# Moving the rows, the activations g, the outputs and the weight temporaries 320 bytes up in SBUF

## The chip, the cores and the metric

The kernel runs on one NeuronCore of a Trainium2 chip. The metric is the device time of one execution in microseconds, lower is better. Three executions of the kernel before took 889.12, 889.74 and 889.91 us; their median, 889.74 us, is the time before. A further execution was taken with the hardware profiler, and the rows further down come from it.

## What is computed

Attention within chunks of 64 positions, followed by a feed-forward layer. All numbers are float32.

```python
scores = q_c @ k_c.T / sqrt(64)          # per batch (8), head (8), chunk of 64 of 576 positions
attn   = exp(scores - max) / (sum + 1e-9)
x      = (attn @ v_c)                    # gathered to [4608 tokens, 512]
h      = x @ w_in                        # w_in  [512, 2048]
g      = h * sigmoid(1.702 * h)
out    = g @ w_out                       # w_out [2048, 512]
```

The weights come in as float64 words of 8 bytes, and the kernel makes float32 values from them itself.

## The kernel before, in words

The 4608 tokens are 36 tiles of 128 rows (`u`), and four tiles make a block (`n`, nine blocks of 512 tokens). The hidden width 2048 is 16 slices of 128 (`j`). The feed-forward part is 9 x 16 = 144 steps (`g = 16 n + j`), all built alike.

To keep float32 accuracy every factor is split in two float32r parts, a high one (`x_h`, `g_h`, plane 0 of `w`) and the rest (`x_l`, `g_l`, plane 1 of `w`), and three products are added. A step therefore has 24 matmuls of 128 x 128 x 512 on TensorE:

- `h_pe` (L606 to L608): four slices `cc` of the model width, three matmuls each, all into one PSUM tile `hp`. The stationary operand, which a weight load (LDWEIGHTS, engine PEld) brings in ahead of each matmul, is a 128-column slice of `w`; the moving operand is `x_l` or `x_h`.
- `g_hi` on ScalarE: L627 applies the activation to `hp` in place, L628 copies it to `g_h`. `g_lo` on VectorE, L632, writes `g_l = hp - g_h`.
- `o_pe` (L641 to L643): four token tiles `t`, three matmuls each, into four PSUM tiles `po`. Here the stationary operand is a 128-column (512-byte) slice of `g_l` or `g_h`, and the moving operand is `w`.

`g_h` and `g_l` have two buffers each, which the steps use in turn. After the last `j` of a block `o_out` copies `po` to `ob` and `o_store` stores it.

The attention of the tiles ahead and the preparation of the weights lie between these matmuls: q and k rows arrive in `rows` or `raw` (`load_rows` L231, `load_qk` L392), weights in `raw_j` (L163, L168). A weight slice passes through a temporary `wtmp` with three buffers (L181, L182 and L188 on VectorE write it, L193 and L196 read it). `s_max` takes the maximum of each score row into a small tile `m` and subtracts it (L451 to L456); `s_sum` makes `z` and `r`.

`Plan.emit` fixes the order of the instructions of all engines from costs written in the kernel, before any tile has an address. The addresses come from tile pools in the order of first use: a pool `const` first, then `two` (two buffers per tag: `xh`, `xl`, `m`, `z`, `r`, `raw`, `gh`, `gl`, `ob`), then `more` (`wtmp`).

Of the kernel before, what the change touches and what calls it, by code (L numbers as in the profile page):

```python
# [9 lines left out]
F32 = mybir.dt.float32  # L10
# [88 lines left out]
def tile_chunk_attention_ffn(  # L99
# [14 lines left out]
    P = 128  # L114
# [15 lines left out]
    two = ctx.enter_context(tc.tile_pool(name="two", bufs=2))  # L130
# [238 lines left out]
    def plan_pair(u):  # L369
# [3 lines left out]
        NG = 2 * NP * 2  # L373

        def bc(a):
            return a.unsqueeze(2).broadcast_to([P, NG, CH])
# [70 lines left out]
        def s_max():  # L447
            sc = st["s"]
            st["e"] = e = const.tile([P, NG, CH], F32, tag="e", name=f"e_{u}")
            m = two.tile([P, NG], F32, tag="m", name=f"m_{u}")  # L450
            nc.vector.tensor_reduce(m, sc, axis=AX.X, op=ALU.max)  # L451
            if pe:
                nc.vector.tensor_tensor(e, sc, bc(m), op=ALU.subtract)
            else:
                split = lambda a: a.rearrange("p (g h) j -> p g h j", h=2)
                nc.vector.tensor_tensor(split(e), sc, split(bc(m)), op=ALU.subtract)  # L456
# [96 lines left out]
        for t in range(2):  # L553
# [5 lines left out]
            PE, 2.4 if pe else 1.4, rank + 0.6, s_pe, need=need, make=ev("s"), take=["att", "att"], give=["tr"],  # L559
        )  # L560
        plan.add(DVE, 2.46, rank + 0.6, s_max, need=[ev("s")], make=ev("m"), take=["e"], give=["att", "att"])
        plan.add(ACT, 1.05, rank + 0.6, s_exp, need=[ev("m")], make=ev("ex"), table="exp")
        plan.add(DVE, 1.65, rank + 0.6, s_sum, need=[ev("ex")], make=ev("z"))
# [180 lines left out]
```

## Time and profile before

| What | Value |
|---|---|
| Median of three runs | 889.74 us |
| Profiled execution, its own time | 889.83 us |
| Span of that execution in the trace | 888.1 us |
| Time outside the span | 1.7 us |
| TensorE busy | 870.6 us, 98% |
| VectorE busy | 389.8 us, 44% |
| ScalarE busy | 317.6 us, 36% |
| GpSimd busy | 32.4 us, 4% |

The span is the time from the first to the last instruction of the program that the profiler saw. Matmuls are pipelined and their ends are modelled, so the time that a matmul takes from the stream is read from the distance between the starts of two matmuls, not from its listed length.

### The profile page before, as it was taken

How to read it: one execution, taken by the hardware profiler on the slowest of the kernel's cores; microseconds unless marked ns; L12 is line 12 of the kernel's file. 1: busy time of each engine (PE TensorE's matmuls, PEld its weight loads, DVE VectorE, ACT ScalarE, POOL GpSimd, SP SyncE). 2: the span in 40 equal slices, each digit the busy share in tenths (PEclk: the TensorE clock that was granted, in tenths of full speed). 3: DMA queues.
4: the chain of work that ended last, by engine and by line, in shares of the span. 5: the costliest groups of instructions: out<-in, count | busy, mean ns of one | idle time of the engine just before them, and what ended most of it. 6: DMA issues, size and time to landing. Idle time of an engine off the chain costs nothing.

```text
span 888.1 us, 14202 instructions
## 1 busy us (share of the span) xinstructions
PE 870.6 (98%) x5882; PEld 705.6 (79%) x5882; DVE 389.8 (44%) x511; ACT 317.6 (36%) x459; POOL 32.4 (4%) x24
## 2 busy tenths in 40 slices
PE   6799999999999999999999999999999999999998
PEld 5587888888888888888888888888888888888886
DVE  5899975277716153433535171617151411111111
ACT  3999653253423223232423241324232322222221
POOL 1000000011000000000000000000000000000000
PEclk9699999999999999999999999999999999999999
DMA  9995244233442313221222031102010110001001
GB/s 238 311 323 169 47 73 98 38 54 67 82 86 54 54 25 76 45 48 25 69 39 49 16 92 25 25 1 71 2 25 1 32 40 1 0 1 48 1 0 48
DMA packets 194592, 55.47 MB, mean 62 GB/s; under 512 B 179680, under 2 KB 187872, under 8 KB 194528
## 3 DMA queue, kind: packets, MB, share of 16 engines
q1 hardware_dynamic: 194528, 54.57, 26.3%
q8 instruction: 46, 0.75, 0.4%
q14 instruction: 18, 0.15, 0.1%
HBM read 45.09 MB, written 9.44 MB: 61 GB/s over the span
## 4 chain that ended last, share of the span: by engine, by line
PE 94%; SPq 2%; DMA 2%; ACT 1%; issue 0%; DVE 0%; ACTq 0%
PE po L641 16%; PE po L642 15%; PE po L643 15%; PE hp L608 15%; PE hp L607 15%; PE hp L606 15%; PE s L443 2%; PE x L503 2%; SPq L231 1%; DMA raw<-in_moe_w_in_dram 1%; DMA rows<-in_k_dram 1%; ACT raw L172 0%; PE qkTp L410 0%; SPq L168 0%; SPq L163 0%
## 5 line engine op out<-in xcount | busy, mean ns | idle before, releaser
L632 DVE TENSOR_TENSOR g_l<-hp,g_h 128x512 fp32r<-128x512 f32 x144 | 99.3, 690 | 413.3 <-ACT g_h L628 412.7
L641 PE MATMUL po<-w,g_l 128*128 128x512 f32 x576 | 232.1, 403 | 0.1
L628 ACT ACTIVATE g_h<-hp 128x512 fp32r<-128x512 f32 x144 | 86.3, 599 | 404.3 <-PE po L643 403.6
L642 PE MATMUL po<-w,g_h 128*128 128x512 f32 x576 | 227.7, 395 | 0.0
L643 PE MATMUL po<-w,g_h 128*128 128x512 f32 x576 | 227.7, 395 | 0.0
L608 PE MATMUL hp<-x_h,w 128*128 128x512 f32 x572 | 225.2, 394 | 0.0
L607 PE MATMUL hp<-x_h,w 128*128 128x512 f32 x572 | 223.9, 391 | 0.0
L606 PE MATMUL hp<-x_l,w 128*128 128x512 f32 x572 | 223.9, 391 | 0.0
L643 PEld LDWEIGHTS po<-w,g_h 128*128 128x128 f32 x576 | 108.6, 189 | 26.3
L641 PEld LDWEIGHTS po<-w,g_l 128*128 128x128 f32 x576 | 108.2, 188 | 25.4 <-DVE g_l L632 0.9
L606 PEld LDWEIGHTS hp<-x_l,w 128*128 128x128 f32 x572 | 107.8, 189 | 25.0
L642 PEld LDWEIGHTS po<-w,g_h 128*128 128x128 f32 x576 | 109.0, 189 | 23.5
L607 PEld LDWEIGHTS hp<-x_h,w 128*128 128x128 f32 x572 | 107.4, 188 | 25.1
L608 PEld LDWEIGHTS hp<-x_h,w 128*128 128x128 f32 x572 | 107.3, 188 | 23.6 <-DVE w L196 0.2
L627 ACT ACTIVATE hp<-hp 128x512 f32<-128x512 f32 x144 | 84.3, 585 | 72.6 <-PE hp L608 67.6
L490 DVE STREAM_TRANSPOSE eT<-e 32x512 f32<-32x512 f32 x112 | 78.7, 702 | 21.0 <-PE x L503 17.2
L470 POOL TENSOR_TENSOR e<-e,r 128x1024 f32<-128x1024 f32 x14 | 26.7, 1906 | 611.4 <-DVE r L466 325.5
L425 DVE STREAM_TRANSPOSE qkT<-raw 128x1024 f32<-128x1024 f32 x28 | 34.7, 1241 | 13.8 <-PE s L443 11.3
L515 ACT ACTIVATE x_h<-x 128x512 fp32r<-128x512 f32 x32 | 17.5, 595 | 33.2 <-PE x L503 33.1
L459 ACT ACT_TABLE_LOAD x16 | 20.5, 1283 | 19.0 <-DVE e L456 18.3
L463 DVE TENSOR_REDUCE z<-e 128x16 f32<-128x1024 f32 x16 | 19.5, 1218 | 9.5 <-ACT e L459 8.8
L443 PEld LDWEIGHTS s<-qkT 64*64 64x64 f32 x1024 | 18.2, 135 | 5.8 <-issue 5.8
(64 smaller groups left out, 412.2 us busy)
## 6 DMA issues: line engine op xcount, KB each, us to landing
out_dram<-ob SPq DMA_DIRECT2D x36, 256.0 KB, 2.1
raw<-in_moe_w_in_dram SPq DMA_DIRECT2D x16, 512.0 KB, 7.3
raw<-in_moe_w_out_dram SPq DMA_DIRECT2D x16, 512.0 KB, 8.0
v<-in_v_dram SPq DMA_DIRECT2D x28, 256.0 KB, 3.3
raw<-in_q_dram SPq DMA_DIRECT2D x144, 32.0 KB, 2.1
raw<-in_k_dram SPq DMA_DIRECT2D x144, 32.0 KB, 2.1
raw<-in_q_dram SPq DMA_DIRECT2D x48, 24.0 KB, 1.9
raw<-in_k_dram SPq DMA_DIRECT2D x48, 24.0 KB, 1.9
```

The costliest lines, as they stand in the source:

```text
L425: nc.vector.transpose(st["tr"][:, i].rearrange("p n (t j) -> p (n t) j", j=32), st["raw"][:, i].rearrange("p n t j -> p (n t) j"),)
L443: nc.tensor.matmul(o, tr[r, 0, n, cols], tr[r, 1, n, cols], start=True, stop=True)
L490: nc.vector.transpose(st["et"][po : po + 32, :, 32 * a : 32 * a + 32], st["e"][pi : pi + 32, :, 32 * b : 32 * b + 32],)
L606: nc.tensor.matmul(hp, wh, xl, start=cc == 0, stop=False)
L607: nc.tensor.matmul(hp, wh, xh, start=False, stop=False)
L608: nc.tensor.matmul(hp, wl, xh, start=False, stop=cc == NCC - 1)
L627: nc.scalar.activation(h_t[g], h_t[g], AF.Gelu_apprx_sigmoid)
L628: nc.scalar.activation(gh, h_t[g], AF.Copy)
L632: nc.vector.tensor_tensor(gl, h_t.pop(g), gh.bitcast(F32), op=ALU.subtract)
L641: nc.tensor.matmul(po, gl[:, c], w[:, 0, :], start=j == 0, stop=False)
L642: nc.tensor.matmul(po, gh[:, c], w[:, 0, :], start=False, stop=False)
L643: nc.tensor.matmul(po, gh[:, c], w[:, 1, :], start=False, stop=j == NF - 1)
```

## The change

The tile `m` of the paired tiles (`plan_pair`) asks for 56 columns in place of 16, and only its first 16 are used. That makes each of its two buffers 160 bytes per partition longer.

```diff
         def s_max():
             sc = st["s"]
             st["e"] = e = const.tile([P, NG, CH], F32, tag="e", name=f"e_{u}")
-            m = two.tile([P, NG], F32, tag="m", name=f"m_{u}")
+            m = two.tile([P, NG + 40], F32, tag="m", name=f"m_{u}")
+            m = m[:, :NG]
             nc.vector.tensor_reduce(m, sc, axis=AX.X, op=ALU.max)
```

The built program has the same 7171 instructions before and after, in the same order on each engine, with the same shapes and the same waits and semaphore updates. What differs is where some tiles start within each partition, in bytes:

| Tile (buffers) | Before | After |
|---|---|---|
| `w`, `raw_j`, the first tiles' `first_a`, `first_b` | 1664 + multiples of 8192 | the same |
| `qkT`, `v`, `e`, `eT` | 116352, 140928, 145024, 149120 | the same |
| `x_h`, `x_l` | 153216, 161408; 169600, 177792 | the same |
| `m` | 185984, 186048 | 185984, 186208 |
| `z`, `r` | 186112, 186176; 186240, 186304 | 320 higher |
| `rows` / `raw` | 186368, 194560 | 186688, 194880 |
| `g_h` | 202752, 204800 | 203072, 205120 |
| `g_l` | 206848, 208896 | 207168, 209216 |
| `ob` | 210944, 212992 | 211264, 213312 |
| `wtmp` | 215040, 219136, 223232 | 215360, 219456, 223552 |

From `rows` on, the moved tiles started at multiples of 2048 bytes (`rows` at 186368 = 91 x 2048); the unmoved ones from `w` to `x_l` start 128 bytes past a multiple of 512. After the change the moved tiles start 320 bytes past a multiple of 2048, which is 64 bytes past a multiple of 128 and of 256.

## Rows read from the trace of the kernel before

**Rows 1.** The page: the span and the instructions.

```profile
span 888.1 us, 14202 instructions
```

**Rows 2.** Windows: length, busy time (count) by engine, clock, DMA share, GB/s.

```profile
41.00:120.00 79.00, 78.69 (x586) 63.91 (x585) 74.81 (x83) 64.00 (x77) 0.00 (x0) 1.00 0.62 175
120.00:700.00 580.00, 580.00 (x4083) 468.67 (x4082) 254.36 (x341) 185.83 (x276) 26.68 (x14) 1.00 0.23 47
700.00:888.00 188.00, 184.35 (x854) 149.37 (x852) 32.35 (x48) 42.69 (x73) 0.00 (x0) 1.00 0.05 18
```

**Rows 3.** The page: the chain that ended last, by engine.

```profile
PE 94%; SPq 2%; DMA 2%; ACT 1%; issue 0%; DVE 0%; ACTq 0%
```

**Rows 4.** Waits: who waited for whom, us in total, times, longest.

```profile
DVE g_l L632 <- ACT g_h L628: 412.7, 102, 4.9
ACT g_h L628 <- PE po L643: 403.6, 122, 4.4
```

**Rows 5.** Timeline of TensorE, one step and the next's end: start, length, instruction.

```profile
764.61 0.40 PE L641 MATMUL po<-w,g_l 128*128 128x512 f32 x1
...
765.55 0.39 PE L642 MATMUL po<-w,g_h 128*128 128x512 f32 x1
765.78 0.39 PE L643 MATMUL po<-w,g_h 128*128 128x512 f32 x1
...
766.24 0.40 PE L642 MATMUL po<-w,g_h 128*128 128x512 f32 x1
766.48 0.40 PE L643 MATMUL po<-w,g_h 128*128 128x512 f32 x1
766.72 0.40 PE L606 MATMUL hp<-x_l,w 128*128 128x512 f32 x1
...
768.11 0.39 PE L641 MATMUL po<-w,g_l 128*128 128x512 f32 x1
...
768.81 0.39 PE L606 MATMUL hp<-x_l,w 128*128 128x512 f32 x1
...
770.17 0.40 PE L641 MATMUL po<-w,g_l 128*128 128x512 f32 x1
...
775.73 0.40 PE L641 MATMUL po<-w,g_l 128*128 128x512 f32 x1
```

**Rows 6.** Groups by line and shape: count, busy us, mean ns, idle before.

```profile
L642 PEld LDWEIGHTS po<-w,g_h 128*128 128x128 f32 x576 | 109.0, 189 | 23.5
...
L606 PEld LDWEIGHTS hp<-x_l,w 128*128 128x128 f32 x572 | 107.8, 189 | 25.0
...
L632 DVE TENSOR_TENSOR g_l<-hp,g_h 128x512 fp32r<-128x512 f32 x144 | 99.3, 690 | 413.3 <-ACT g_h L628 412.7
L628 ACT ACTIVATE g_h<-hp 128x512 fp32r<-128x512 f32 x144 | 86.3, 599 | 404.3 <-PE po L643 403.6
...
L518 DVE TENSOR_TENSOR x_l<-x,x_h 128x512 fp32r<-128x512 f32 x32 | 20.6, 684 | 2.9 <-ACT x_h L515 2.8
...
L196 DVE TENSOR_TENSOR w<-wtmp,w 128x1024 fp32r<-128x1024 f32 x16 | 19.4, 1215 | 0.4 <-ACT w L193 0.4
...
L515 ACT ACTIVATE x_h<-x 128x512 fp32r<-128x512 f32 x32 | 17.5, 595 | 33.2 <-PE x L503 33.1
L456 DVE TENSOR_TENSOR e<-s,m 128x1024 f32<-128x1024 f32 x14 | 17.1, 1225 | 0.5
```

**Rows 7.** DMA issues: transfer, queue, count, KB each, median us to landing.

```profile
first_a<-in_k_dram SPq DMA_DIRECT2D x4, 256.0 KB, 5.1
...
rows<-in_k_dram SPq DMA_DIRECT2D x3, 256.0 KB, 5.6
```

**Rows 8.** The chain in order of time, 13 to 41 us: start, length, what.

```profile
18.04 9.14 DMA raw<-in_moe_w_in_dram
...
27.19 6.47 DMA rows<-in_k_dram
33.67 1.19 ACT raw L172
```

## The prediction

> **What bounds the kernel now.** I read the page first for the span [rows 1], 888.1 us. The profiled execution took 889.83 us, so 1.7 us lie outside the span, and it stands 0.09 us above the median of 889.74 us.
>
> Then the windows [rows 2]. From 41 us on TensorE is busy without a break that counts: 78.69 of 79 us, 580.00 of 580, and 184.35 of the last 188, where only the end of the kernel is missing. The granted clock is 1.00, its upper level of 2.4 GHz, in all three stretches. VectorE and ScalarE are busy for 74.81 and 64.00 us of the first of them, but for only 254.36 and 185.83 us of the 580. The chain that ended last [rows 3] says the same: 94% of it is TensorE. The reader should see that in some 95% of the span only a change in the pace of the matmul stream can move the end.
>
> The waits [rows 4] show on which side the slack is. The copy to `g_h` (L628) waited for the matmuls of `o_pe` 122 times, 403.6 us in total, 3.3 us each, because both `g` buffers were still being read. VectorE's L632 then waited 412.7 us in 102 times for L628, 4.0 us each. So the two instructions that write `g` have microseconds to spare in a step.
>
> Last the pace itself, from starts on TensorE's timeline [rows 5]. The step shown runs from 764.61 to 770.17 us, 5.56 us for 24 matmuls, 231.7 ns each; 144 steps of that are 800.6 us. In that step the nine matmuls of `o_pe` for three token tiles take 764.61 to 766.72 and the three of the fourth 768.11 to 768.81: 2.81 us for 12, 234.2 ns each. The twelve of `h_pe` take the rest, 2.75 us, 229.2 ns each. The next step, which reads the other pair of `g` buffers 2048 bytes away, takes 770.17 to 775.73, 5.56 us again.
>
> **The change part by part.** *What it adds and removes.* No instruction, wait or order changes, and the extra 40 columns of `m` are never written or read. L451 and L456 keep their shapes. So the sum of added and removed work is 0.0 us, and all that is left is what an address costs. Some operands start 320 bytes higher. I go through who touches them.
>
> *Weight loads of `g`* (1728 in all: 144 steps x 4 tiles x 3). This is the only moved operand on the path that sets the end. Before, a slice of `g` starts at a multiple of 512 bytes and a slice of `w` starts 128 bytes past one. The load of `g_h` takes 189 ns on average and that of `w` for L606 also 189 ns [rows 6]. A slice of `w` crosses a 512-byte and a 256-byte boundary, a slice of `g` crosses neither, and no difference shows. After the change a slice of `g` starts 64 bytes past a multiple of 128; no operand of the three main loops stands so in the trace of before, so this case is not covered by a row. It is bounded below by the equal 189 ns (cost 0), and it is nearest to that row, because one shift of the start has already been seen to cost nothing. I take 0.0 us. Cover: the load lies under the matmul ahead of it, 231.7 ns long, so it could grow by about 43 ns before the stream had to wait. The idle time ahead of these loads says the same: 23.5 us over 576 [rows 6], 41 ns each.
>
> *Writes of `g`* by L628 and L632. The same operations onto unmoved tiles that start 128 bytes past a multiple of 512: L515 onto `x_h` 595 ns against 599 for L628, L518 onto `x_l` 684 ns against 690 for L632 [rows 6]. Both ends differ by 6 ns or less, 1%, with no sign that an aligned start is better. Even 10% of both, 0.13 us a step, would disappear in the waits of 3.3 and 4.0 us [rows 4]. If that cover were gone, L641 would start late by the growth: 144 x 0.13 = 19 us. The cover is some 25 times the cost. 0.0 us.
>
> *`wtmp`, `z`, `r`.* L196 reads the aligned `wtmp` and the unmoved `w` and takes 1215 ns for 1024 elements; L456 writes the unmoved `e` in 1225 ns [rows 6]. Again start addresses of two kinds and one price. These operations matter only while the weights are prepared, up to about 120 us, where VectorE is busy for 74.81 of 79 us [rows 2]. 0.0 us, with 1% of that stretch's VectorE time, 0.7 us, as the end to keep.
>
> *Transfers.* Rows go in pieces of 256 bytes per head. Into `first_a`, which starts 128 bytes past a multiple of 256, the k rows landed in 5.1 us; into `rows`, which starts on a multiple, in 5.6 us [rows 7]. The less aligned target is not the slower one, though both figures come from a crowded queue. Later rows and stores lie beside 580 us of unbroken matmuls; DMA is busy for 0.23 of that stretch [rows 2], so a longer transfer has room. One transfer of rows is on the chain: 6.47 us from 27.19 to 33.67 us, after which ScalarE goes on with a weight [rows 8]. I take 0.0 us for it too.
>
> Sum: 889.83 + 0.0 for the profiled execution, and, 0.09 lower, **889.7 us** for the median.
>
> **A rule against it.** The Trainium skill, page "DMA: Bandwidth & Descriptors", section "How a descriptor splits into AXI transactions", says that a piece which does not start on a 256-byte boundary has its first transaction start at the boundary below, and the bytes ahead of it cost beats too. A 256-byte piece that starts 64 bytes past a boundary would by that need 10 beats of 32 bytes where an aligned one needs 8 (an estimate from the page), and the sum would be that of the third rival below, 891.3 us. By the rows above, where 128 bytes off the boundary cost nothing (5.1 against 5.6 us), the rule does not show.
>
> **The rivals.**
>
> 1. *Slower: the load of `g` becomes longer than the matmul above it.* The place is TensorE's weight load ahead of L641 to L643. If memory is read in pieces of 128 bytes, a 512-byte slice that starts 64 bytes past such a piece touches five pieces instead of four: 189 x 5/4 = 236 ns. It decides once the load passes some 232 ns, the present distance between starts. At 236 ns, 4.3 ns too long, 1728 loads add 7.4 us: 897.1 us. If the 43 ns between a load's end and the next matmul were still needed on top, the distance would be 279 ns and the addition 47 x 1728 = 82 us. Nothing in the trace shows a step of this kind, and the equal 189 ns speak against it; no row excludes a grain of 128 bytes.
>
> 2. *Faster: the slower pace of `o_pe` comes from the address of `g`.* Its matmuls stand 234.2 ns apart and those of `h_pe` 229.2 [rows 5]. If the aligned start of `g` were the reason, and the move removed it, 1728 x 5.0 ns = 8.6 us would go: 881.1 us. For it: the moving operands of both are unmoved and alike in their alignment, and `g` is what differs. Against it: the same instruction on the same buffer, L642, takes 0.23 us from 765.55 to 765.78 and 0.24 us from 766.24 to 766.48, and L606 to L608 need 1.39 us for six from 766.72 and 1.36 us for six from 768.81 [rows 5]. The pace differs with the place in the step as much as between the two kinds. `o_pe` also changes its output tile every three matmuls, which explains a loss as well.
>
> 3. *Slightly slower: rows arrive late at the start.* After the move 64 of the 256 bytes of each piece lie past a 256-byte boundary. If they had to be moved apart, and cost their share of the bytes once more, a quarter, the 6.47 us of rows on the chain [rows 8] would become 8.1 us, and the stream would start 1.6 us later: 891.3 us. For it: those rows are waited for. Against it: the equal landings of [rows 7]. This stays within what can be told from no change.
>
> **How the numbers follow.** A difference of 0.2% (1.8 us) is about what a measurement of this kernel can tell from no change; the three runs spread by 0.8 us. No cost from an address: 0.66. Rival 3 with some of its price: 0.06, inside the 0.2%, near its edge. Rival 1: 0.12, most of it for a growth that just passes the cover. Rival 2: 0.11, most of it for a part of the 5.0 ns. The remaining 0.05 goes evenly to small effects of either sign that I cannot name a place for. Faster 0.13, same 0.72, slower 0.15. The range holds the whole of "same" and the small ends of rivals 1 and 2: one nanosecond on each of the 1728 matmuls of `o_pe` is 1.7 us, and I go to 1.7 ns either way, 3.0 us: 886.7 to 892.7 us.
>
> **What would show it right or wrong.** Right: 5.56 us from L641 to L641 in the late steps; loads of `g` at 188 to 189 ns; L628 and L632 within 1% of 599 and 690 ns; L628's wait for L643 still near 400 us; the first L172 that ends the chain's wait for rows at about 33.7 us. Rival 1 would show as loads of `g` above 230 ns and a longer L641 to L641. Rival 2 would show as `o_pe` at 229 ns a matmul, and a step of 5.50 us. Rival 3 would show as the same steps, all some 1.6 us later. The prediction is wrong if the step changes by more than 12 ns, since 144 x 12 ns is 1.8 us.

## The result and the profile after

The kernel after the change takes 879.76 us (median of four runs, 879.57 to 879.82) against 889.83 us (four runs, 889.12 to 890.10). The ratio is 0.9886, with a 95% interval of 0.9873 to 0.9898: 10.1 us faster. The forecast was no change, 889.7 us, with a range down to 886.7. It was wrong.

The diff adds one line, so lines behind it have a number one higher: `h_pe` is now L607 to L609, `g_h` is written by L629, `g_l` by L633, and `o_pe` is L642 to L644.

The page of the profiled execution (879.57 us, 1.8 us of them outside the span):

```profile
span 877.8 us, 14202 instructions
```

Windows of the kernel after, columns as in [rows 2]:

```profile
41.00:120.00 79.00, 78.70 (x589) 64.23 (x588) 75.33 (x84) 64.12 (x78) 0.00 (x0) 1.00 0.65 176
120.00:700.00 580.00, 580.00 (x4170) 472.95 (x4169) 259.38 (x349) 187.99 (x281) 26.66 (x14) 1.00 0.23 47
```

TensorE is busy throughout, as before [rows 2], at the same granted clock of 1.00, but 4170 matmuls start in the 580 us where 4083 did. The busy time cannot show the change, the count can.

TensorE's timeline of the kernel after, one late step, columns as in [rows 5]:

```profile
739.89 0.39 PE L642 MATMUL po<-w,g_l 128*128 128x512 f32 x1
...
741.95 0.39 PE L607 MATMUL hp<-x_l,w 128*128 128x512 f32 x1
...
743.31 0.39 PE L642 MATMUL po<-w,g_l 128*128 128x512 f32 x1
...
744.00 0.39 PE L607 MATMUL hp<-x_l,w 128*128 128x512 f32 x1
...
745.35 0.39 PE L642 MATMUL po<-w,g_l 128*128 128x512 f32 x1
```

The step takes 5.46 us where it took 5.56 [rows 5]. The twelve matmuls of `o_pe` (739.89 to 741.95 and 743.31 to 744.00) take 2.75 us, 229 ns each, down from 234. The six of `h_pe` that follow the nine of `o_pe` take 1.36 us instead of 1.39, and the six later ones 1.35 instead of 1.36, although no operand of `h_pe` moved against another. Over all starts between 120 and 880 us, without distances above 260 ns, at which attention lies between, the mean distance (the average of the three lines of each) fell from 233.7 to 229.3 ns in `o_pe` and from 229.6 to 227.4 ns in `h_pe`. Applied to all of them, that is 1728 x 4.4 ns + 1716 x 2.2 ns = 11.4 us, an estimate, near the 10.3 us by which the span became shorter.

Groups by line of the kernel after, columns as in [rows 6]:

```profile
L643 PEld LDWEIGHTS po<-w,g_h 128*128 128x128 f32 x576 | 108.3, 188 | 20.7
...
L607 PEld LDWEIGHTS hp<-x_l,w 128*128 128x128 f32 x572 | 107.4, 188 | 24.1 <-DVE g_l L633 0.2
L633 DVE TENSOR_TENSOR g_l<-hp,g_h 128x512 fp32r<-128x512 f32 x144 | 99.2, 689 | 404.5 <-ACT g_h L629 403.9
L629 ACT ACTIVATE g_h<-hp 128x512 fp32r<-128x512 f32 x144 | 86.1, 598 | 395.9 <-PE po L644 395.1
```

None of these durations moved by more than 1 ns against [rows 6]. The time that left the matmul stream is in no instruction's length.

Waits of the kernel after, and its transfers of k rows, columns as in [rows 4] and [rows 7]:

```profile
DVE g_l L633 <- ACT g_h L629: 403.9, 102, 4.8
ACT g_h L629 <- PE po L644: 395.1, 121, 4.3
```

```profile
first_a<-in_k_dram SPq DMA_DIRECT2D x4, 256.0 KB, 5.1
...
rows<-in_k_dram SPq DMA_DIRECT2D x3, 256.0 KB, 6.2
```

The waits shrink with the step and stay long. The rows land later than before, 6.2 against 5.6 us [rows 7]. The chain of the kernel after in the same stretch as [rows 8]:

```profile
30.84 1.17 PE x L329 x32
...
32.53 0.58 ACT raw L176
...
33.61 1.20 ACT raw L172
...
40.67 0.50 PE po L642
```

The transfer of rows is no longer on it, and L172 starts at 33.61 us as it did at 33.67. The first matmul of `o_pe` starts at 40.67 us against 40.69 before. All of the gain lies behind that point. Step 16 begins its `o_pe` at 147.40 us before and 146.66 after, step 119 at 753.49 and 745.35, step 143 at 881.40 and 871.11: 0.7 us until step 16, 7.4 us in the next 103 steps, most of which have attention between their matmuls, and 2.2 us in the last 24, which have none.

### The profile page after: what moved, and what is told of

It reads as the page before. It is cut to its first block, busy times and chain, and to the rows that moved or that the text cites. A ratio compares the mean times of both kernels' runs of the same rounds, so it can differ in the third digit from the quotient of the medians.

```text
span 877.8 us, 14202 instructions
## 1 busy us (share of the span) xinstructions
PE 860.0 (98%) x5882; PEld 703.2 (80%) x5882; DVE 389.7 (44%) x511; ACT 317.7 (36%) x459; POOL 32.3 (4%) x24
## 4 chain that ended last, share of the span: by engine, by line
PE 94%; SPq 2%; ACT 1%; DMA 1%; DVE 1%; issue 1%; POOL 0%; ACTq 0%; DVEq 0%; POOLq 0%
PE po L642 16%; PE po L643 15%; PE po L644 15%; PE hp L607 15%; PE hp L608 15%; PE hp L609 15%; PE s L443 2%; PE x L504 2%; SPq L231 1%; DMA raw<-in_moe_w_out_dram 1%; ACT raw L172 1%; PE qkTp L410 0%; ACT raw L176 0%; ACT w L193 0%; POOL first_b L308 0%
## 5 line engine op out<-in xcount | busy, mean ns | idle before, releaser
L633 DVE TENSOR_TENSOR g_l<-hp,g_h 128x512 fp32r<-128x512 f32 x144 | 99.2, 689 | 404.5 <-ACT g_h L629 403.9
L642 PE MATMUL po<-w,g_l 128*128 128x512 f32 x576 | 229.5, 398 | 0.1
L629 ACT ACTIVATE g_h<-hp 128x512 fp32r<-128x512 f32 x144 | 86.1, 598 | 395.9 <-PE po L644 395.1
L643 PE MATMUL po<-w,g_h 128*128 128x512 f32 x576 | 226.9, 394 | 0.0
L644 PE MATMUL po<-w,g_h 128*128 128x512 f32 x576 | 224.3, 389 | 0.0
L607 PE MATMUL hp<-x_l,w 128*128 128x512 f32 x572 | 223.6, 391 | 0.0
L609 PE MATMUL hp<-x_h,w 128*128 128x512 f32 x572 | 222.9, 390 | 0.2 <-DVE w L196 0.2
L608 PE MATMUL hp<-x_h,w 128*128 128x512 f32 x572 | 223.1, 390 | 0.0
L642 PEld LDWEIGHTS po<-w,g_l 128*128 128x128 f32 x576 | 108.1, 188 | 25.6 <-DVE g_l L633 0.9
L644 PEld LDWEIGHTS po<-w,g_h 128*128 128x128 f32 x576 | 108.2, 188 | 24.3
L607 PEld LDWEIGHTS hp<-x_l,w 128*128 128x128 f32 x572 | 107.4, 188 | 24.1 <-DVE g_l L633 0.2
L609 PEld LDWEIGHTS hp<-x_h,w 128*128 128x128 f32 x572 | 107.4, 188 | 23.5 <-DVE w L196 0.8
L608 PEld LDWEIGHTS hp<-x_h,w 128*128 128x128 f32 x572 | 107.4, 188 | 22.6
L643 PEld LDWEIGHTS po<-w,g_h 128*128 128x128 f32 x576 | 108.3, 188 | 20.7
```

Source lines behind the costliest of these rows:

```text
L607: nc.tensor.matmul(hp, wh, xl, start=cc == 0, stop=False)
L608: nc.tensor.matmul(hp, wh, xh, start=False, stop=False)
L609: nc.tensor.matmul(hp, wl, xh, start=False, stop=cc == NCC - 1)
L629: nc.scalar.activation(gh, h_t[g], AF.Copy)
L633: nc.vector.tensor_tensor(gl, h_t.pop(g), gh.bitcast(F32), op=ALU.subtract)
L642: nc.tensor.matmul(po, gl[:, c], w[:, 0, :], start=j == 0, stop=False)
```

## The experiments

**Theories.** Rival 2 of the prediction had named the place, the pace of `o_pe`, so I began with what about `g` could do it. A: the start of `g` by itself. R: the distance in SBUF between the operand that is being loaded (`g`) and the one that streams at the same time (`w`), modulo some period. O: one of the other moved tiles. All kernels of this section have the 14202 instructions of before in their traces, in the same order on each engine; only addresses differ.

**e1_g_alone.** `g` moves, everything else keeps its alignment modulo 2048.

```diff
     more = ctx.enter_context(tc.tile_pool(name="more", bufs=NTMP))
+    gap = ctx.enter_context(tc.tile_pool(name="gap", bufs=1))
+    gp = ctx.enter_context(tc.tile_pool(name="gp", bufs=2))
+    gap.tile([P, 80], F32, tag="gap", name="gap")
...
-            gh = two.tile([P, BT], F32R, tag="gh", name=f"g_h_{g}")
-            gl = two.tile([P, BT], F32R, tag="gl", name=f"g_l_{g}")
+            gh = gp.tile([P, BT], F32R, tag="gh", name=f"g_h_{g}")
+            gl = gp.tile([P, BT], F32R, tag="gl", name=f"g_l_{g}")
```

> The four g buffers are put in a pool of their own at the end of SBUF and start 320 bytes past a multiple of 2048, as after the change; m has its old size and rows, z, r, outputs and weight temporaries keep their alignment of before. Theory A (where g itself starts) expects about 880 us and steps of 5.46 us. Theory R (the distance of g from the w that streams at the same time, modulo some period) expects the same, 880. Theory O (one of the other moved tiles) expects 890 us and steps of 5.56 us.

Measured: 879.77 us, ratio 0.9886 (0.9872 to 0.9901). The window from 120 to 700 us of this run:

```profile
120.00:700.00 580.00, 579.98 (x4170) 472.86 (x4169) 259.59 (x348) 188.19 (x281) 26.69 (x14) 1.00 0.23 47
```

The same 4170 matmuls as after the change. Moving `g` alone gives the whole of the effect.

**e2_all_but_g.** The pool of e1 with a gap of 176 columns, and the changed `m`.

```diff
-    gap.tile([P, 80], F32, tag="gap", name="gap")
+    gap.tile([P, 176], F32, tag="gap", name="gap")
...
-            m = two.tile([P, NG], F32, tag="m", name=f"m_{u}")
+            m = two.tile([P, NG + 40], F32, tag="m", name=f"m_{u}")
+            m = m[:, :NG]
```

> The reverse: rows, z, r, outputs and weight temporaries start 320 bytes higher, g starts at a multiple of 1024 as before. A and R expect about 890 us, O expects 880 us.

Measured: 889.89 us, ratio 1.0001 (0.9992 to 1.0011). Theory O falls.

**e3_everything.** A gap ahead of all tiles of the kernel before.

```diff
+    low = ctx.enter_context(tc.tile_pool(name="low", bufs=1))
+    low.tile([P, 80], F32, tag="low", name="low")
     const = ctx.enter_context(tc.tile_pool(name="const", bufs=1))
```

> An unused gap of 320 bytes ahead of every tile moves all of SBUF up alike: g starts where it starts after the change, 320 past a multiple of 2048, but w and x move with it, so that all distances are those of before. A expects 880 us, R expects 890 us.

Measured: 889.88 us, ratio 1.0000 (0.9991 to 1.0010). Its window:

```profile
120.00:700.00 580.00, 580.00 (x4083) 468.74 (x4082) 254.39 (x341) 185.91 (x276) 26.70 (x14) 1.00 0.23 47
```

`g` starts where it does after the change, at the same address to the byte, and the 4083 matmuls are those of before [rows 2]. Theory A falls.

**e4_w_not_g.** The pool and gap of e1, and the `low` pool of e3 with 176 columns.

```diff
-    low.tile([P, 80], F32, tag="low", name="low")
+    low.tile([P, 176], F32, tag="low", name="low")
```

> w, x and all else move 704 bytes up and g 1024: g starts at a multiple of 1024 as before, while its distance from w is that of after the change (320 bytes more than before). A expects 890 us, R expects 880 us.

Measured: 879.78 us, ratio 0.9886 (0.9871 to 0.9900). Its window:

```profile
120.00:700.00 580.00, 580.00 (x4170) 472.99 (x4169) 259.55 (x348) 188.28 (x281) 26.69 (x14) 1.00 0.24 47
```

The alignment of `g` is that of before, the distance that of after, and the time that of after. R stands, and A is refuted from both sides. `w` and `x` keep their places against each other in these four runs, so they do not yet tell whether the distance of `g` from `w` or from `x` counts; e6 does.

One more rival can be read from the trace of before: that not the loads of `g` but the writes of it disturb the stream. In the step of [rows 5] they are these:

```profile
769.07 0.60 ACT L628 ACTIVATE g_h<-hp 128x512 fp32r<-128x512 f32 x1 [3.67 <-PE po L643]
769.70 0.69 DVE L632 TENSOR_TENSOR g_l<-hp,g_h 128x512 fp32r<-128x512 f32 x1 [4.87 <-ACT g_h L628]
```

They lie beside the six quicker matmuls of `h_pe` (768.81 to 770.17, 1.36 us) and reach only 0.22 us into the slow ones of `o_pe` that follow. So the writes are not what slows the rest of those.

**e5, the period.** The kernel e1 with gaps of 16, 32, 64 and 128 columns in place of 80, so that `g` alone moves by 64, 128, 256 and 512 bytes; the edit for 128 bytes is shown.

```diff
-    gap.tile([P, 80], F32, tag="gap", name="gap")
+    gap.tile([P, 32], F32, tag="gap", name="gap")
```

> Only g is moved, by 64 bytes. Theory R, now with a period: the extra time hangs on the distance of g from w modulo P. 320 bytes changed it and 1024 did not, so P divides 1024 but not 320: 128, 256, 512 or 1024. With 128 or 256 a move by 64 is the same as one by 320: about 880 us. With 512 or 1024 it is a new distance (448 past a multiple of 512) and may lie anywhere from 874 to 892 us.

> Only g is moved, by 128 bytes. P = 128 expects 890 us as before. P = 512 puts the slices of g a multiple of 512 bytes from the start of w, which is the distance that the fast matmuls of h_pe (227 ns) have between w and x: the matmuls of o_pe should then also stand 227 ns apart, and the time be about 876 us.

> Only g is moved, by 256 bytes. P = 128 or 256 expects 890 us as before; P = 512 or 1024 is a new distance (128 past a multiple of 512), from 874 to 892 us.

> Only g is moved, by 512 bytes. P = 128, 256 or 512 expects 890 us and the same distances between starts, to the nanosecond, as before; P = 1024 expects another time.

Measured: 64 bytes 880.22 us (two runs, ratio 0.9890, 0.9861 to 0.9919); 128 bytes 874.77 us (two runs, 0.9829, 0.9800 to 0.9857); 256 bytes 889.71 us (1.0002, 0.9991 to 1.0014); 512 bytes 889.84 us (0.9999, 0.9988 to 1.0010). Moves by 64 and by 320 bytes agree within 0.5 us, moves by 0, 256, 512 and (e2) 1024 within 0.2 us: the period is 256 bytes in all that was tried. Of my four candidates 128 is excluded, since 128 bytes is not like 0, and with 512 or 1024 two or more different distances would have to give the same time by chance. The best distance of the four is a multiple of 256. The forecast of 876 us for it was near, but it had been made for a period of 512, which is not what these runs show.

**e6_x_off.** Is only `g` concerned, or any loaded operand and the one that streams beside it? In `h_pe` `w` is loaded and `x` streams.

```diff
+    mid = ctx.enter_context(tc.tile_pool(name="mid", bufs=1))
+    mid.tile([P, 32], F32, tag="mid", name="mid")
     two = ctx.enter_context(tc.tile_pool(name="two", bufs=2))
```

> A gap of 128 bytes between w and x: x and everything above it, g too, lie 128 bytes higher. So g stands at the best distance from w found so far (as in the run with g alone moved by 128, 874.8 us), but x is now 128 past a multiple of 256 from w, where g was before the change. If any load is slowed by the operand that streams beside it at that distance, the matmuls of h_pe now stand some 234 ns apart, and the time is about 887 to 890 us. If only g is special, it stays at 874.8 us and 227 ns.

Measured: 887.35 us, ratio 0.9967 (0.9955 to 0.9979). The timeline shows where (this kernel has `h_pe` at L608 to L610 and `o_pe` from L643):

```profile
743.07 0.40 PE L608 MATMUL hp<-x_l,w 128*128 128x512 f32 x1
...
744.46 0.39 PE L643 MATMUL po<-w,g_l 128*128 128x512 f32 x1
...
745.15 0.40 PE L608 MATMUL hp<-x_l,w 128*128 128x512 f32 x1
...
746.54 0.39 PE L643 MATMUL po<-w,g_l 128*128 128x512 f32 x1
...
747.24 0.39 PE L643 MATMUL po<-w,g_l 128*128 128x512 f32 x1
...
748.60 0.40 PE L608 MATMUL hp<-x_l,w 128*128 128x512 f32 x1
```

The six matmuls of `h_pe` that follow three of `o_pe` (745.15 to 746.54) take 1.39 us instead of the 1.36 of [rows 5], and the nine of `o_pe` (746.54 to 748.60) 2.06 us instead of 2.11. Of these nine the first three take 0.70 us, 233 ns each, and the other six 1.36 us, 227 ns each. The six of `h_pe` that follow the nine (743.07 to 744.46) take 1.39 us, as they did before. So the disturbance has moved from `o_pe` to `h_pe` with the distance of 128 bytes, and part of it reaches into the first matmuls behind. Over all starts the mean is 232.0 ns in `h_pe`, where I had expected 234, and 229.4 in `o_pe`, where I had expected 227; the time fell inside the 887 to 890 us. The run also tells `w` from `x`: `g` still lies 128 past a multiple of 256 from `x`, as before, and yet most of `o_pe` runs at 227 ns. What counts there is `g` against `w`.

**e7_m_16.** The change itself with 16 columns in place of 40, which puts `g` 128 bytes higher.

```diff
-            m = two.tile([P, NG + 40], F32, tag="m", name=f"m_{u}")
+            m = two.tile([P, NG + 16], F32, tag="m", name=f"m_{u}")
```

> The change itself with 16 columns more for m in place of 40: g and what else lies above m move by 128 bytes. The distance theory expects what g alone moved by 128 gave, 874.8 us, 15 us under the time before and 5 under that of the change.

Measured: 874.98 us, ratio to before 0.9831 (0.9818 to 0.9845): 14.9 us faster than before, and 4.8 us faster than the change. Its timeline (lines as after the change) and window:

```profile
739.10 0.39 PE L607 MATMUL hp<-x_l,w 128*128 128x512 f32 x1
...
740.46 0.39 PE L642 MATMUL po<-w,g_l 128*128 128x512 f32 x1
...
742.50 0.39 PE L607 MATMUL hp<-x_l,w 128*128 128x512 f32 x1
...
745.90 0.39 PE L642 MATMUL po<-w,g_l 128*128 128x512 f32 x1
```

```profile
120.00:700.00 580.00, 579.98 (x4185) 475.59 (x4184) 260.15 (x350) 189.24 (x283) 26.66 (x14) 1.00 0.23 47
```

`o_pe`: nine matmuls from 740.46 to 742.50, 2.04 us, 227 ns each. `h_pe`: six from 739.10 to 740.46, 1.36 us, 227 ns each. The step is 5.44 us and all its distances are alike.

**e8, between the steps of 64.** The kernel e1 with gaps of 48 and 40 columns: `g` alone moves by 192 and 160 bytes.

```diff
-    gap.tile([P, 80], F32, tag="gap", name="gap")
+    gap.tile([P, 40], F32, tag="gap", name="gap")
```

> Only g is moved, by 192 bytes: it starts 64 past a multiple of 256 from w. If the cost hangs on how far the start is from a multiple of 256, whichever way, it is that of a move by 64 or 320: 880 us. If it hangs on the sign too, it differs; below 874.8 us if 0 is not the best distance.

> Only g is moved, by 160 bytes: 32 past a multiple of 256 from w. If memory counts in units of 64 bytes this is as good as a move by 128, 874.8 us, or as bad as one by 192; if the cost rises evenly it lies between the two.

Measured: 192 bytes 888.90 us (0.9987, 0.9977 to 0.9998); 160 bytes 890.45 us (1.0006, 0.9996 to 1.0016). For 192 bytes the second of my readings holds: the cost depends on the sign. 64 bytes below a multiple of 256 cost 5 us against the best, 64 above it 14 us. For 160 bytes neither 874.8 us nor an even rise came true; the nearest of what I had offered is "as bad as one by 192", and it came out some 1.5 us worse still. 32 above costs as much as 128.

All runs by their distances, each worked out from the starts (after the change, for example, 203072 - 1664 = 786 x 256 + 192):

| Runs | g from w, modulo 256 | x from w, modulo 256 | us |
|---|---|---|---|
| e5_g_128, e7_m_16 | 0 | 0 | 874.77, 874.98 |
| e8_g_160 | 32 | 0 | 890.45 |
| e8_g_192 | 64 | 0 | 888.90 |
| before, e2, e3, e5_g_256, e5_g_512 | 128 | 0 | 889.83, 889.89, 889.88, 889.71, 889.84 |
| after, e1, e4, e5_g_64 | 192 | 0 | 879.76, 879.77, 879.78, 880.22 |
| e6_x_off | 0 | 128 | 887.35 |

## Why the prediction was wrong, step by step

- **What bounds the kernel** was right: the pace of the matmul stream. The step fell by 0.10 us and the kernel followed, with no other engine in the way.
- **The step that failed is the cost of the weight loads of `g`, "I take 0.0 us".** I priced an address by the listed duration of the instruction that uses it, and found 189 ns for `w` and for `g`. Those durations were 187 to 188 ns in `o_pe` at the worst distance too (e8_g_160). What the addresses changed is how closely the matmul stream runs, while the listed lengths of the loads stay within 1 ns: 233.7 ns a matmul before, 229.3 after, 227 in e7_m_16. I compared loads of two alignments, but not pairs of a load and a stream, which is what e3 and e4 show to count. One reading under that comparison was false too: a 512-byte slice of `g` that starts at a multiple of 512 does cross a 256-byte boundary, in its middle, as a slice of `w` crosses two.
- **Rival 2 named the right place and nearly the size**, 8.6 us, with a chance of 0.11, but its reason, the aligned start of `g`, is refuted: e3 has the start of after and is slow, e4 has an aligned one and is fast. Of its price 4.4 of the 5.0 ns came in `o_pe`, and 2.2 ns came in `h_pe`, which I had not counted. That its 881.1 us lies 1.3 us from the measured time is in part luck.
- **What I held against rival 2 was a symptom of the same thing.** The uneven pace within a step, L642 at 0.23 and 0.24 us and `h_pe` at 1.39 and 1.36 us [rows 5], goes away in e7_m_16, where nothing but addresses changed. The matmuls of `h_pe` behind the nine of `o_pe` were slow because of `g`, which they do not use: moving `g` alone (e1) gives the means of after, 227.4 ns in `h_pe`. "It differs by place too" was no argument that the address is innocent. Nor was the change of the output tile every three matmuls the reason: `o_pe` changes it in e7_m_16 as before, and stands at 227 ns.
- **Rival 1** did not happen: loads of `g` stayed at 188 ns.
- **The writes of `g`, `wtmp`, `z`, `r` at 0.0 us** were right: 598 and 689 ns for L629 and L633, and e2, which moves all but `g`, is level with before.
- **The transfers at 0.0 us** were right in the sum and wrong in the reason. I had read 5.1 against 5.6 us [rows 7] as "alignment costs nothing". In the runs with `rows` on a multiple of 256 (before, e1, all of e5 and e8) the k rows landed in 5.3 to 5.6 us, in the runs without (after, e2, e3, e4, e6, e7) in 5.9 to 6.2 us. The two rows that I compared are different transfers at different times; the same transfer in two layouts is the comparison that counts. Its direction agrees with the rule of the Trainium skill, page "DMA: Bandwidth & Descriptors", section "How a descriptor splits into AXI transactions". Its size does not: about 0.6 us on 5.4 is 11%, and the estimate of 10 beats for 8 gave a quarter. That section of the Trainium skill speaks of bytes that are fetched, and here it is the target that moved. Rival 3's delay of these transfers exists, with less than half of its price, but it does not reach the end: e1 with aligned rows and the change without are both at 879.8 us.

What stays open: why the cost runs as it does with the distance (0 the fastest, 32, 64 and 128 dear, 192 in between), and whether it is the load or the stream that is held up, since the ends of matmuls are modelled and the listed lengths do not move. Only five distances modulo 256 were tried, 0, 32, 64, 128 and 192, and no other data type or matmul width. That the load must go on at the same time as the stream is argued, not shown: in every run it does.

## What to carry to other kernels

Where a stream of matmuls is the bound, the addresses of the loaded and of the streamed operand can be a tuning knob: here, with float32r operands and 512 columns, placing them a multiple of 256 bytes apart made the kernel 1.7% faster, by 64 unused bytes in each buffer of one small tile. Read the pace from the distance between starts and look whether it is even within a step; an uneven pace without a wait was here the sign of something that busy time and mean durations hide. A kernel change that adds or resizes a small tile can move everything allocated behind it, as it did here, so a gain or loss of 1% after such a change may come from the move alone: pad the tile to the old layout before crediting the change.

## What the hardware showed that I had not expected

- The pace of this load-and-matmul stream depends on the distance between its two operands in SBUF, with a period of 256 bytes in all that was tried: 226.9 to 227.1 ns a matmul of `o_pe` at 0 (e5_g_128), 233.7 ns at 128 (before). The Trainium skill, page "TensorE: Matmul & The Clock Gate", section "Step-by-step: what each phase is for", says that loading the next tile's weights doesn't steal read bandwidth from the running matmul. In this kernel the running matmuls and the loads are not independent of each other at every distance: the pace differs by 3% with where the two operands lie. Whether read bandwidth is what they share, no run shows.
- The pace carries over: matmuls whose own operands keep their distance (`h_pe`, 229.6 to 227.4 ns) became faster when those ahead of them did. In e6_x_off it is the other way about: of nine matmuls of `o_pe` behind a slow `h_pe` the first three stand 233 ns apart and the rest 227.
- Runs with the same distances repeat each other: 4083 matmuls in 580 us before and in e2, e3, e5_g_512; 4170 after and in e1, e4, e5_g_64.
